# Matmuls of 512 and 256 columns for the mixture of a three-stage kernel, and unbroken runs of its scores and values

## The chip, the cores and the metric

The kernel runs on one core of a Trainium2 chip. TensorE (PE) multiplies, VectorE (DVE), ScalarE (ACT) and GpSimd (POOL) do the work around it, and the queue of SyncE (SP) issues the DMAs. The metric is the device time of one execution in microseconds (us); lower is better. All inputs and outputs are float32 in HBM.

## The reference

Three stages follow one another. Attention with a block mask is computed for 4 batches of 8 heads, 576 tokens and a head size of 64; its 512 values per token go through a layer that takes the largest of three products; and the result goes through four weighted experts, for all 2304 tokens.

```python
scores = scale * np.matmul(q, k.transpose(0, 1, 3, 2))      # 4 x 8 heads, 576 x 576
scores = np.where(block_i >= block_j, scores, -1e9)         # blocks of 64 tokens
attn = np.exp(scores - np.max(scores, axis=-1, keepdims=True))
attn = attn / (np.sum(attn, axis=-1, keepdims=True) + 1e-09)
x = np.matmul(attn, v)                                      # laid out as 2304 x 512
h = np.maximum(np.maximum(x @ w1, x @ w2), x @ w3)          # 2304 x 768, "the mixture"
x = h @ w_out                                               # 2304 x 512
p = domain_probs / (domain_probs.sum(-1, keepdims=True) + 1e-09)
for e in range(4):                                          # 1024 wide each
    out += p[:, e:e + 1] * (np.maximum(x @ e_w1[e], 0.0) @ e_w2[e])
```

## The kernel before, in words

Attention goes by pairs of heads: `NPAIR = 4` pairs for each of the 4 batches, so 16 pairs, numbered from 0. For each pair, `scores` (line 123) multiplies queries by keys in three or four steps; the two heads of a pair lie in the two halves of the partitions (`own = (lo, hi)`), so that a score matmul uses 64 of the array's 128 rows (line 144), and the matmuls of the two heads start nearly together. The last 64 queries of both heads are one matmul of all 128 rows (line 159). DVE finds the smallest score of each row (line 173), ACT takes the exponential with its sum (line 180), POOL divides (line 203, in `normalise`, which is issued one step later). `turn_probs` (line 218) transposes the probabilities on TensorE into PSUM (line 231), DVE and ACT copy them out (line 241). `values` (line 245) multiplies them by the values in 20 matmuls, each of which fills 64 of the 128 output columns of the array (line 263), and ACT copies the two results into `xf` (lines 271 and 272).

PSUM tiles of scores, transposes and values of pairs 4 to 15 share one ring of four banks, `ps_x`.

The mixture of a batch is the generator `moe1(b)` (line 426). Each float32 operand is split into a rounded high and a low part, and a product is three matmuls (`mm3`, line 400): high by high, high by low, low by high. For 18 weight tiles of 128x512 (three matrices by six stretches of 128 columns) and for four of the output matrix it goes over the 576 tokens of the batch in two halves of `CH = 288` columns. A run into one PSUM bank is 12 matmuls for the first kind and 18 for the second. One batch is 18 x 2 x 12 + 4 x 2 x 18 = 576 matmuls. DVE takes the maximum (line 443), POOL splits the hidden values (lines 445, 446). The splits of the inputs, `xh` and `xl`, are made by `moe1_inputs` (lines 423, 424) at the end of the batch's last pair.

The mixture of batch b is laid between the attention of batch b+1: after each step of a pair the main loop calls `filler.upto((at - 1) * UNITS - LAG)`, which issues so many units of `moe1` (a unit is the stretch between two `yield`s). Batch 3 has no attention to lie between; its mixture goes on alone, with the first steps of the experts beside it. The mixture of batch 0 converts its weights on the way (`Convert`, from line 295: ACT, POOL and DVE work on each tile, and a DMA writes the result to `held`); later batches load `held` into five buffers `wt` (512 KB a load) and two buffers `wo` (768 KB).

The order of the instructions on each engine is made by the scheduler of the language, from the program's order and its own view of what is ready; `tc.keep_in_program_order` ties an instruction to the one before that was so marked. The order is fixed before the kernel runs: TensorE takes its instructions one after the other, and one that waits holds up all that stand behind it.

The experts (from line 581 on) follow when the mixture of batch 3 is done: the function `save_tails` (line 648) writes columns 384 to 575 of the mixture's outputs to HBM, and `weights_out` (line 742) loads the experts' second matrices.

Of the kernel before, what the change touches and what calls it, by code (L numbers as in the profile page):

```python
# [15 lines left out]
LAG = 10  # L16
# [11 lines left out]
def program(tc, q, k, v, w123, w_out, probs, e_w1, e_w2, out):  # L28
# [10 lines left out]
    CH = S // 2  # L39
# [38 lines left out]
    for _ in range(4):  # L78
        mp.tile([P, S], F32, name="xf", tag="xf", bufs=4)
# [42 lines left out]

    def scores(n, step):
        pair = pairs[n]
        if step == 0:
# [11 lines left out]
        todo = []  # L137
        for i, at, w, tiles_ in STEPS[step]:
            views = []
            for h in range(2):  # L140
                o = at if isinstance(at, int) else at[h]
                views.append(st[tiles_[h]][:, o:o + w])
            for h in (0, 1) if step == 2 else (1, 0):
                ins = nc.tensor.matmul(  # L144
                    out=views[h], lhsT=qs[own[h], P * i:P * i + P], rhs=ks[own[h], 0:w], start=True, stop=not masked,
                )
                if not masked or len(todo) or h == (step == 2):
                    tc.keep_in_program_order(ins)
            for h in range(2):
                if masked:  # L150
# [4 lines left out]
                todo.append((i, h, views[h]))  # L155
        if step >= 2:
            view = st[-1][:, 192:768]
            for c, n_ in ((0, 320), (320, 256)):
                ins = nc.tensor.matmul(  # L159
                    out=view[:, c:c + n_], lhsT=qs[:, QT:QW], rhs=ks[:, c:c + n_], start=True, stop=True  # L160
                )
                if not masked:
                    tc.keep_in_program_order(ins)
            todo.append((4, 0, view))
        todo.sort(key=lambda x: (step == 0) * x[1])
        done, cols = [], list(range(*COLS[step]))
        for c in range(0, len(cols), 2):
            work = list(zip(cols, todo))[c:c + 2]
            for m, (i, h, x) in work:
                if i < 4 and not masked:  # L170
                    nc.vector.memset(x[lo, x.shape[1] - 64:], 1e30)
            for m, (i, h, x) in work:
                nc.vector.tensor_reduce(mn[:, m:m + 1], x, axis=AX.X, op=ALU.min)  # L173
            for m, (i, h, x) in work:
# [5 lines left out]
                exps.append(nc.scalar.activation(  # L180
                    to, x, ACTF.Exp, bias=mn[:, m:m + 1], scale=-1.0, accum_out=sm[:, m:m + 1],
                ))
                done.append((m, i, to))
# [34 lines left out]
    def turn_probs(g, part):  # L218
# [7 lines left out]
        for n in PARTS[part]:  # L226
# [14 lines left out]
            (nc.scalar.copy if n else nc.vector.tensor_copy)(to, tt[:, 0:c])  # L241
# [3 lines left out]
    def values(n):  # L245
        pair = pairs[n]
        eh, e4, vraw = pair["eh"], pair["e4"], pair["vraw"]
        pool, tag = (ps_v, "v") if n < NPAIR else (ps_x, "x")
        pv = [pool.tile([P, 512], F32, name=f"pv{i}", tag=tag) for i in range(2)]
        ins = None  # L250
        for j in range(5):
            for to, of in ((1, 0), (1, 1), (0, 0)):
                if j and to == 0 or j == 4 and of == 0:
                    continue
                for h in (1, 0):
# [11 lines left out]
                    if old is not None:  # L267
                        tc.keep_in_program_order(ins)
        made["pv"] = ins
        xf = pair["xf"] = mp.tile([P, S], F32, name="xf", tag="xf", bufs=4)  # L270
        nc.scalar.copy(xf[:, 0:P], pv[0][:, 0:P])
        nc.scalar.copy(xf[:, P:S], pv[1][:, 0:S - P])

    def weigh(n, behind):
# [8 lines left out]
        nc.vector.tensor_tensor(pair["xf"][:, 0:512], rt, pair["xf"][:, 0:512], op=ALU.mult)  # L283
# [5 lines left out]
    for n, src in enumerate(tiles):  # L289
        A = src.shape[1]  # L290
        step = A if A <= 4 else A // 2
        pieces += [(n, slice(a, a + step)) for a in range(0, A, step)]

    class Convert:
# [14 lines left out]
        def home(self, n):  # L309
            A = tiles[n].shape[1]  # L310

            tag, bufs = ("wo", 2) if n >= 3 * NF or n in (WT, WT + 1) else ("wt", WT)
            return mp.tile([P, 2, A, P], F32R, name=tag, tag=tag, bufs=bufs)
# [72 lines left out]
    def moe_weight(b, n, tag, bufs):  # L386
# [3 lines left out]
        else:  # L390
            A = tiles[n].shape[1]
            wt = mp.tile([P, 2, A, P], F32R, name=tag, tag=tag, bufs=bufs)
# [21 lines left out]
    def moe1_inputs(b, ds):  # L414
        if b not in xs:
            xs[b] = (
                mp.tile([P, KD, S], F32R, name="xh", tag="xh"),
                mp.tile([P, KD, S], F32R, name="xl", tag="xl"),
            )
        xh, xl = xs[b]  # L420
        for d in ds:
            xf = pairs[b * NPAIR + d]["xf"]
            nc.scalar.copy(xh[:, d], xf)
            nc.vector.tensor_tensor(xl[:, d], xf, f(xh[:, d]), op=ALU.subtract)

    def moe1(b):
        xh, xl = xs[b]
        hh = mp.tile([P, NF, S], F32R, name="hh", tag="hh")
        hl = mp.tile([P, NF, S], F32R, name="hl", tag="hl")
        for ff in range(NF):  # L430
            prev = [None, None]
            for n in range(3):
                wh, wl = moe_weight(b, 3 * ff + n, "wt", WT)
                for c in range(2):
                    cs = slice(c * CH, (c + 1) * CH)
                    m = ps_m.tile([P, 512], F32, name="m", tag="m")
                    yield from mm3(m[:, 0:CH], [(wh[:, d], wl[:, d], xh[:, d, cs], xl[:, d, cs]) for d in range(KD)])
                    t = prev[c]
                    if t is None:
                        t = prev[c] = mp.tile([P, CH], F32, name="mt", tag="mt", bufs=3)  # L440
                        nc.scalar.copy(t, m[:, 0:CH])
                    else:
                        nc.vector.tensor_tensor(t, m[:, 0:CH], t, op=ALU.max)  # L443
                    if n == 2:
                        nc.gpsimd.tensor_scalar(hh[:, ff, cs], t, 1.0, 0.0, op0=ALU.mult, op1=ALU.add)
                        nc.gpsimd.tensor_tensor(hl[:, ff, cs], t, f(hh[:, ff, cs]), op=ALU.subtract)
                    yield
        for d in range(KD):
            wh, wl = moe_weight(b, 3 * NF + d, "wo", 2)
            for c in range(2):  # L450
                cs = slice(c * CH, (c + 1) * CH)
                m = ps_m.tile([P, 512], F32, name="m", tag="m")
                yield from mm3(m[:, 0:CH], [(wh[:, ff], wl[:, ff], hh[:, ff, cs], hl[:, ff, cs]) for ff in range(NF)])
                nc.scalar.copy(x2f[b][:, d, cs], m[:, 0:CH])
                yield
# [794 lines left out]
```

## Time and profile before

| | us |
|---|---|
| median of 3 runs | 1239.15 |
| lowest and highest | 1237.73, 1239.34 |
| the profiled execution | 1239.25 |
| its span, first to last instruction | 1237.1 |
| TensorE busy | 1209.7 (98%) |
| DVE, ACT, POOL busy | 824.2, 455.6, 289.8 |

The profile is one execution. A busy matmul in it is counted until its result has drained, and matmuls overlap, so the busy share says that TensorE hardly stood still, not that each matmul was as short as it can be. How long a matmul holds the array is read from the time between its start and the next one's. The granted clock is a share of 2.4 GHz.

### The profile page before, as it was taken

To read this page: it belongs to the slowest core of one execution; us is meant where nothing else is said; L and a number is where in the kernel's file an instruction comes from. 1 tells how busy PE (TensorE), PEld (TensorE's weight loads), DVE (VectorE), ACT (ScalarE), POOL (GpSimd) and SP (SyncE) were. 2 spreads that over 40 slices of the span, in tenths; PEclk is the share of its full clock that TensorE was granted. 3 is DMA by queue.
4 is the path that set the end of the run, shared out by engine and by line. 5 is a ranking of instruction groups with operands and counts; after the bars stand their busy time and mean duration, and the time that the engine had idled before them with its cause. 6 is when DMAs were issued, how large, how long until landed. Compare 5 with 4: busy or idle time off the path is not lost.

```text
span 1237.1 us, 19744 instructions
## 1 busy us (share of the span) xinstructions
PE 1209.7 (98%) x7681; PEld 1119.4 (90%) x7681; DVE 824.2 (67%) x1453; ACT 455.6 (37%) x964; POOL 289.8 (23%) x360
## 2 busy tenths in 40 slices
PE   7799999999999999999999999999999999999998
PEld 4468888888888999999999998999999999999998
DVE  5756674434333544478888895768787888586896
ACT  6765555334333421333444450233232223222222
POOL 3447663334233022342433440000000000000000
PEclk8899999999999999999999999999999999999999
DMA  7635575443433487679887864867888887676664
GB/s 269 226 113 186 170 249 170 147 138 119 138 116 103 129 299 271 223 289 334 315 311 285 326 239 149 315 252 296 331 301 317 317 312 267 251 267 225 251 214 168
DMA packets 82352, 290.75 MB, mean 235 GB/s; under 512 B 8716, under 2 KB 18004, under 8 KB 69204
## 3 DMA queue, kind: packets, MB, share of 16 engines
q1 hardware_dynamic: 82260, 289.51, 66.1%
q8 instruction: 60, 0.98, 0.3%
q14 instruction: 32, 0.26, 0.1%
HBM read 206.34 MB, written 83.14 MB: 234 GB/s over the span
## 4 chain that ended last, share of the span: by engine, by line
PE 88%; DVE 3%; DMA 3%; ACT 2%; POOL 2%; issue 1%; SPq 0%; DVEq 0%; ACTq 0%; POOLq 0%
PE m L761 26%; PE m L405 24%; PE o L920 17%; PE pv L263 3%; PE o L843 3%; PE o L847 3%; PE o L846 3%; PE st L144 3%; PE tt L231 3%; PE m L920 2%; PE st L159 1%; ACT p L180 1%; DMA w<-kb 1%; DMA arena<-in_w 1%; DVE mn L173 1%
## 5 line engine op out<-in xcount | busy, mean ns | idle before, releaser
L405 PE MATMUL m<-xh,wt 128*128 128x288 f32 x1120 | 246.1, 303 | 0.0
L761 PE MATMUL m<-t,w 128*128 128x384 f32 x1152 | 227.8, 336 | 0.0
L920 PE MATMUL o<-hx,w 128*128 128x384 f32 x1176 | 226.1, 337 | 0.5 <-DMA w<-kb 0.5
L920 PEld LDWEIGHTS o<-hx,w 128*128 128x128 f32 x1176 | 207.9, 188 | 0.8 <-PE m L761 0.8
L761 PEld LDWEIGHTS m<-t,w 128*128 128x128 f32 x1152 | 203.4, 188 | 2.4
L405 PEld LDWEIGHTS m<-xh,wt 128*128 128x128 f32 x1120 | 184.2, 188 | 10.8 <-issue 6.3
L761 PE MATMUL m<-b,w 128*128 128x384 f32 x864 | 175.2, 336 | 2.2 <-ACT tmp L786 1.6
L405 PE MATMUL m<-xl,wt 128*128 128x288 f32 x560 | 164.9, 294 | 0.0
L761 PEld LDWEIGHTS m<-b,w 128*128 128x128 f32 x864 | 153.0, 188 | 5.9 <-ACT tmp L786 1.9
L405 PEld LDWEIGHTS m<-xl,wt 128*128 128x128 f32 x560 | 105.3, 188 | 0.3
L180 ACT ACTIVATE p<-st,mn 128x128 f32<-128x128 f32 (+2 forms) x144 | 78.3, 554 | 63.1 <-DVE mn L173 62.9
L443 DVE TENSOR_TENSOR mt<-m,mt 128x288 f32<-128x288 f32 x96 | 42.8, 452 | 88.0 <-PE m L405 87.7
L781 DVE TENSOR_TENSOR tmp<-m,tmp 128x384 f32<-128x384 f32 x144 | 77.9, 549 | 19.5 <-PE m L761 19.1
L173 DVE TENSOR_REDUCE mn<-st 128x1 f32<-128x128 f32 (+2 forms) x144 | 70.0, 515 | 30.5 <-PE st L151 15.5
L203 POOL TENSOR_SCALAR p<-p,sm 128x128 f32<-128x128 f32 (+4 forms) x112 | 65.1, 600 | 101.0 <-ACT e L241 45.2
L405 PE MATMUL m<-hh,wo 128*128 128x288 f32 x384 | 81.2, 299 | 0.3 <-DMA wo<-held 0.2
L891 ACT CAST hx<-hq 128x768 fp32r<-128x768 f32 x49 | 40.6, 836 | 99.0 <-PE o L920 74.4
L843 PE MATMUL o<-w,hh 128*128 128x512 f32 x192 | 74.7, 391 | 0.2 <-ACT hh L821 0.2
L846 PE MATMUL o<-w,hh 128*128 128x512 f32 x192 | 74.6, 390 | 0.0
L847 PE MATMUL o<-w,hl 128*128 128x512 f32 x192 | 74.4, 391 | 0.0
L231 PE MATMUL tt<-ident,p 128*128 128x128 f32 x400 | 60.7, 282 | 11.0 <-ACT p L180 6.1
L716 POOL TENSOR_TENSOR w<-part,w 128x512 fp32r<-128x512 f32 x32 | 49.5, 1568 | 88.1 <-ACT w L714 68.3
(143 smaller groups left out, 1886.9 us busy)
## 6 DMA issues: line engine op xcount, KB each, us to landing
w<-kb SPq DMA_DIRECT2D x55, 1024.0 KB, 6.0
w<-ka SPq DMA_DIRECT2D x30, 1792.0 KB, 8.3
ka<-w SPq DMA_DIRECT2D x16, 1792.0 KB, 6.7
wt<-held SPq DMA_DIRECT2D x54, 512.0 KB, 4.0
kb<-part SPq DMA_DIRECT2D x16, 1024.0 KB, 6.9
kb<-w SPq DMA_DIRECT2D x16, 768.0 KB, 4.8
arena<-in_w SPq DMA_DIRECT2D x18, 512.0 KB, 3.8
wo<-held SPq DMA_DIRECT2D x12, 768.0 KB, 4.4
```

Source lines behind the costliest of these rows:

```text
L173: nc.vector.tensor_reduce(mn[:, m:m + 1], x, axis=AX.X, op=ALU.min)
L180: exps.append(nc.scalar.activation(to, x, ACTF.Exp, bias=mn[:, m:m + 1], scale=-1.0, accum_out=sm[:, m:m + 1],))
L203: normal.append(nc.gpsimd.tensor_scalar(x, x, sm[:, c:c + 1], 1.0, op0=ALU.mult, op1=ALU.mult))
L231: nc.tensor.transpose(tt[:, c:c + P], pt[i][:, k0:k0 + P], ident)
L405: nc.tensor.matmul(out=out_, lhsT=w, rhs=x, start=m == 0, stop=m == n - 1)
L716: eng.tensor_tensor(w[:, a:b, 1], raw[:, a:b], f(w[:, a:b, 0]), op=ALU.subtract)
L761: ins = nc.tensor.matmul(out=m, lhsT=a, rhs=b, start=start and n == 0, stop=stop and n == 3 * KH - 1, skip_group_check=True,)
L781: nc.vector.tensor_tensor(t, x, y, op=ALU.add)
L843: ins = nc.tensor.matmul(out=o, lhsT=hh[:, ts], rhs=wh, start=i == 0, stop=False)
L846: nc.tensor.matmul(out=o, lhsT=hh[:, ts], rhs=wl, start=False, stop=False)
L847: nc.tensor.matmul(out=o, lhsT=hl[:, ts], rhs=wh, start=False, stop=i == G - 1)
L920: nc.tensor.matmul(out=o, lhsT=a, rhs=b, start=start and m == 0, stop=stop and m == 2, skip_group_check=True,)
```

## The change

The mixture no longer halves the 576 tokens of a batch. It goes over the first `MAIN = 512` in one run; the last `REST = 64` tokens of each batch are split by `moe1_inputs` into tiles `rest_x` that hold all four batches (256 columns), and `moe1(3)` multiplies them beside batch 3's own 512: each weight tile of batch 3 is used for a run of 512 and then a run of 256. Their hidden values lie in `rest_h` and in two buffers that were weight buffers (`wu`), so batch 3 takes weights into `wt` (three) and `wo` (two). `xf` has no tile of its own any more: it lies in the part of `arena` that will hold batch 3's outputs. `mm3` yields after 4 matmuls and not after 6, and `UNITS` and `LAG` follow.

For pairs 4 to 15, the first matmul of a step of scores and of a pair's values gets added dependencies (`whole`): on the instructions that empty the PSUM banks which all of the run will need (`busy`, and `c_ends` for the wide score tile), and for the values on all copies of the transposed probabilities (`turned`). The rest of the run is issued under `tc.high_priority()`.

```diff
-LAG = 10
+LAG = 9
...
+    MAIN = 512
+    REST = S - MAIN
     for x in ("xh", "xl"):
-        mp.tile([P, KD, S], F32R, name=x, tag=x)
-    hidden = [mp.tile([P, NF, S], F32R, name=x, tag=x) for x in ("hh", "hl")]
+        mp.tile([P, KD, MAIN], F32R, name=x, tag=x)
...
+    rest_x = [mp.tile([P, KD, B * REST], F32R, name=f"rx{i}", tag=f"rx{i}") for i in range(2)]
+    rest_h = mp.tile([P, 2, 2, B * REST], F32R, name="rh", tag="rh")
...
+    XB = 4
+    x_ends, c_ends = [], []
+
+    def whole(ins, ends):
+        for x in ends:
+            tc.add_manual_dep(
+                ins.ins, x.ins.name, mybir.DependencyInfo(mybir.DependencyClass.Sync, mybir.DependencyReason.DATA),
+                reason="a run begins when all of it can",
+            )
+
+    def busy(count):
+        at = len(x_ends)
+        return [x for n in range(max(0, at - XB), at + count - XB) for x in x_ends[n]]
+
     def scores(n, step):
         pair = pairs[n]
+        before = busy(KINDS[step].count("x")) + (c_ends[-1] if c_ends and "c" in KINDS[step] else [])
...
+                if n >= NPAIR and not todo and h == (step != 2):
+                    whole(ins, before)
+                    rest.enter_context(tc.high_priority())
...
+        before = busy(2) + pair["turned"]
         pv = [pool.tile([P, 512], F32, name=f"pv{i}", tag=tag) for i in range(2)]
...
+                    elif n >= NPAIR:
+                        whole(ins, before)
+                        rest.enter_context(tc.high_priority())
+        rest.close()
         made["pv"] = ins
-        xf = pair["xf"] = mp.tile([P, S], F32, name="xf", tag="xf", bufs=4)
...
+        xf = pair["xf"] = x2f[B - 1][:, n % NPAIR]
...
+            if b == B - 1 and not wide and n % WT >= 3:
+                wide = True
+                taken[0] += 1
+            wt = weight_tile(n, wide)
             nc.sync.dma_start(out=f(wt[:].rearrange("p k a f -> p k (a f)")), in_=held[n][:, :, 0:A * P])
...
-                if m % 6 == 0 and m < n:
+                if m % 4 == 0 and m < n:
                     yield
 
-    UNITS = 3 * NF * 2 * 2 + KD * 2 * 3
+    UNITS = 3 * NF * 3 + KD * 5
...
         for d in ds:
             xf = pairs[b * NPAIR + d]["xf"]
-            nc.scalar.copy(xh[:, d], xf)
-            nc.vector.tensor_tensor(xl[:, d], xf, f(xh[:, d]), op=ALU.subtract)
+            rs = slice(b * REST, (b + 1) * REST)
+            for cs, h, l in (
+                (slice(0, MAIN), xh[:, d], xl[:, d]), (slice(MAIN, S), rest_x[0][:, d, rs], rest_x[1][:, d, rs]),
+            ):
+                nc.scalar.copy(h, xf[:, cs])
+                nc.vector.tensor_tensor(l, xf[:, cs], f(h), op=ALU.subtract)
...
+        runs = [(MAIN, "mt", *xs[b], *hs, lambda d: x2f[b][:, d, 0:MAIN])]
+        if b == B - 1:
+            room = [rest_h] + [mp.tile([P, 2, 2, B * REST], F32R, name="wu", tag="wu", bufs=2) for _ in range(2)]
+            hs = [[x[:, i, j] for x in room for j in range(2)] for i in range(2)]
+            runs.append((B * REST, "mr", *rest_x, *hs, lambda d: whole[:, d, :, MAIN:S]))
         for ff in range(NF):
-            prev = [None, None]
+            prev = [None] * len(runs)
             for n in range(3):
-                wh, wl = moe_weight(b, 3 * ff + n, "wt", WT)
-                for c in range(2):
-                    cs = slice(c * CH, (c + 1) * CH)
-                    m = ps_m.tile([P, 512], F32, name="m", tag="m")
-                    yield from mm3(m[:, 0:CH], [(wh[:, d], wl[:, d], xh[:, d, cs], xl[:, d, cs]) for d in range(KD)])
+                wh, wl = moe_weight(b, 3 * ff + n)
+                for c, (w, tag, xh, xl, hh, hl, _) in enumerate(runs):
+                    m = ps_m.tile([P, 512], F32, name="m", tag="m")[:, 0:w]
+                    yield from mm3(m, [(wh[:, d], wl[:, d], xh[:, d], xl[:, d]) for d in range(KD)])
```

How the instructions stand on TensorE around the values of pair 9, in the attention of batch 2: `pv` is the values' result, `m` a run of the mixture, `tt` a tile of transposes, `st` scores. Before:

```order
L263 MATMUL pv_2909<-e_2623,vraw 64x64 x2
L263 MATMUL pv_2909<-eh,vraw 64x256 x2
L405 MATMUL m<-xh,wt 128x288
...
L405 MATMUL m<-xh,wt 128x288
L263 MATMUL pv_2909<-e_2623,vraw 64x64 x2
L263 MATMUL pv_2909<-eh,vraw 64x128 x2
L263 MATMUL pv_2909<-e_2623,vraw 64x64 x4
L405 MATMUL m<-xh,wt 128x288
```

And now (line 292 is what line 263 was, 452 is 405, 257 is 231, 165 is 144):

```order
L452 MATMUL m<-xh,wu 128x512
L292 MATMUL pv_2423<-eh,vraw 64x384 x2
L292 MATMUL pv_2423<-e_2224,vraw 64x64 x2
L292 MATMUL pv_2422<-eh,vraw 64x128 x2
L292 MATMUL pv_2423<-eh,vraw 64x384 x2
L292 MATMUL pv_2423<-e_2224,vraw 64x64 x2
L292 MATMUL pv_2423<-eh,vraw 64x256 x2
L292 MATMUL pv_2423<-e_2224,vraw 64x64 x2
L292 MATMUL pv_2423<-eh,vraw 64x128 x2
L292 MATMUL pv_2423<-e_2224,vraw 64x64 x4
L257 MATMUL tt<-ident,p_2380 128x128 x4
```

The 12 matmuls of the mixture that stood inside the values are gone from there, and the transposes of the next pair follow the values at once.

TensorE where batch 1's attention ends and the mixture of batch 1 begins. Before:

```order
L263 MATMUL pv_2218<-e_1880,vraw 64x64 x4
L405 MATMUL m<-hl,wo 128x288
...
L231 MATMUL tt<-ident,p_2134 128x128 x4
...
L405 MATMUL m<-hl,wo 128x288
...
L144 MATMUL st<-raw 128x128 x2
```

And now:

```order
L292 MATMUL pv_1911<-e_1649,vraw 64x64 x4
L257 MATMUL tt<-ident,p_1850 128x128 x4
L257 MATMUL tt<-ident,p_1698 128x128
L257 MATMUL tt<-ident,p_1696 128x128
L257 MATMUL tt<-ident,p_1698 128x128 x2
L165 MATMUL st<-raw 128x128 x2
L165 MATMUL st<-raw 128x384 x2
L257 MATMUL tt<-ident,p_1858 128x128 x2
L452 MATMUL m<-xh,wt 128x512 x2
L257 MATMUL tt<-ident,p_1863 128x128 x4
L452 MATMUL m<-xl,wt 128x512
```

Before, the output products of batch 0 (`hl,wo`) stood between these; now none is left, and the first matmuls after the values are two of batch 1's mixture that need the high part of its last pair.

The queue of SP at the end of the mixture of batch 3: `wo<-held` loads an output weight tile, `xt` is what `save_tails` writes, `part` is the first load of an expert's second matrix. Before:

```order
L393 DMA wo<-held_97 128x1536
L653 DMA xt_4897<-arena 128x2x192
L393 DMA wo<-held_98 128x1536
L653 DMA xt_4897<-arena 128x2x192
L653 DMA xt_4899<-arena 128x2x192
L745 DMA part<-in_e_w 128x1024
```

And now:

```order
L440 DMA wo<-held_97 128x1536
L708 DMA xt_3893<-arena 128x2x192
L708 DMA xt_3894<-arena 128x2x192
L440 DMA wo<-held_98 128x1536
L708 DMA xt_3893<-arena 128x2x192
L708 DMA xt_3894<-arena 128x2x192
L708 DMA xt_3895<-arena 128x2x192
L708 DMA xt_3896<-arena 128x2x192
L800 DMA part<-in_e_w 128x1024
```

Four of the eight writes stood in the attention of batch 2 before; now all eight stand here, six of them ahead of the load of `part`.

## Rows read from the trace of the kernel before

**Rows 1.** Busy time by stage: us, PE DVE ACT POOL, clock, DMA share, GB/s

```profile
77.00:419.00 342.00, 341.82 (x2662) 299.14 (x2659) 162.48 (x380) 151.38 (x414) 145.00 (x218) 1.00 0.47 149
...
107.00:137.00 30.00, 29.91 (x232) 25.57 (x231) 18.96 (x38) 16.09 (x42) 21.07 (x27) 1.00 0.52 174
```

**Rows 2.** Timeline of TensorE in batch 3's output products: start, us, instruction

```profile
424.01 0.29 PE L405 MATMUL m<-hl,wo 128*128 128x288 f32 x1
...
426.79 0.30 PE L405 MATMUL m<-hl,wo 128*128 128x288 f32 x1
```

**Rows 3.** Timeline of TensorE in the experts, 512 columns

```profile
559.16 0.39 PE L843 MATMUL o<-w,hh 128*128 128x512 f32 x1
...
562.56 0.39 PE L843 MATMUL o<-w,hh 128*128 128x512 f32 x1
```

**Rows 4.** Timeline of TensorE around broken values, pair 13

```profile
362.75 0.29 PE L405 MATMUL m<-xh,wt 128*128 128x288 f32 x1
362.96 0.87 PE L263 MATMUL pv<-eh,vraw 128*64 128x384 f32 x4
...
364.75 0.60 PE L263 MATMUL pv<-eh,vraw 128*64 128x256 f32 x4
365.29 0.41 PE L405 MATMUL m<-xh,wt 128*128 128x288 f32 x1
365.53 0.30 PE L405 MATMUL m<-xl,wt 128*128 128x288 f32 x1
```

**Rows 5.** Timeline of TensorE, values of pairs 1 and 3, no mixture beside

```profile
47.56 0.87 PE L263 MATMUL pv<-eh,vraw 128*64 128x384 f32 x4
...
74.81 0.87 PE L263 MATMUL pv<-eh,vraw 128*64 128x384 f32 x4
...
76.60 0.60 PE L263 MATMUL pv<-eh,vraw 128*64 128x256 f32 x4
77.04 0.28 PE L263 MATMUL pv<-e,vraw 128*64 128x64 f32 x4
...
77.37 0.40 PE L263 MATMUL pv<-e,vraw 128*64 128x64 f32 x8
77.70 0.66 PE L280 MATMUL rt<-ident,arena 128*128 128x128 f32 x4
78.20 1.04 PE L231 MATMUL tt<-ident,p 128*128 128x128 f32 x8
```

**Rows 6.** Timeline of TensorE, scores of pair 14 and the next mixture run

```profile
357.13 1.56 PE L144 MATMUL st<-raw 64*128 64x512 f32 x8
...
359.51 0.48 PE L405 MATMUL m<-xh,wt 128*128 128x288 f32 x1
```

**Rows 7.** Timeline of POOL after these scores

```profile
364.87 3.01 POOL L203 TENSOR_SCALAR p<-p,sm 128x512 f32<-128x512 f32 x5 [0.42 <-DVE sm L188]
```

**Rows 8.** Groups by shape: busy us, mean ns, idle before

```profile
L203 POOL TENSOR_SCALAR p<-p,sm 128x512 f32<-128x512 f32 x24 | 17.1, 723 | 15.2 <-DVE sm L188 12.7 <-ACT arena L331 1.8 <-ACT eh L241 0.6
...
L241 ACT COPY eh<-tt 128x512 f32<-128x512 f32 x32 | 18.8, 587 | 21.1 <-PE tt L231 21.1
...
L272 ACT COPY xf<-pv 128x448 f32<-128x448 f32 x16 | 8.6, 536 | 24.6 <-PE pv L263 24.6
```

**Rows 9.** Chain of waits while batch 0's weights are converted: start, us, what

```profile
100.01 2.10 POOL p L203 x3
...
109.25 0.33 PE tt L231
```

**Rows 10.** Chain of waits at the end of batch 3's mixture

```profile
494.55 4.65 DMA wo<-held
499.34 9.79 PE m L405 x72
509.13 3.14 PE m L761 x18
```

**Rows 11.** Timeline of SP's queue there

```profile
505.24 0.46 SPq L745 DMA_DIRECT2D part<-in_e_w  x1
```

More of the change, by code (lines that the diff above doesn't have):

```diff
@@ L121, in program @@
     COLS = ((0, 4), (4, 6), (6, 9), (4, 9))
+    XB = 4
[9 more added lines that the diff above has]
+        return [x for n in range(max(0, at - XB), at + count - XB) for x in x_ends[n]]
     def scores(n, step):
         pair = pairs[n]
+        before = busy(KINDS[step].count("x")) + (c_ends[-1] if c_ends and "c" in KINDS[step] else [])
+        ends = [[] for _ in KINDS[step]]
+        for x, end in zip(KINDS[step], ends):
+            (x_ends if x == "x" else c_ends).append(end)
         if step == 0:
@@ L154, in scores @@
                     ))
-                todo.append((i, h, views[h]))
+                todo.append((i, h, views[h], ends[tiles_[h]]))
         if step >= 2:
@@ L182, in scores @@
                 ))
+                end.append(exps[-1])
                 done.append((m, i, to))
@@ L240, in turn_probs @@
                 to = pair["eh"][h][:, o:o + w].rearrange("x s c -> x (s c)")
-            (nc.scalar.copy if n else nc.vector.tensor_copy)(to, tt[:, 0:c])
+            x_ends.append([(nc.scalar.copy if n else nc.vector.tensor_copy)(to, tt[:, 0:c])])
+            pair.setdefault("turned", []).append(x_ends[-1][0])
         if part == 1 and h == 0:
@@ L268, in values @@
                         tc.keep_in_program_order(ins)
+                    elif n >= NPAIR:
+                        whole(ins, before)
+                        rest.enter_context(tc.high_priority())
+        rest.close()
         made["pv"] = ins
-        xf = pair["xf"] = mp.tile([P, S], F32, name="xf", tag="xf", bufs=4)
-        nc.scalar.copy(xf[:, 0:P], pv[0][:, 0:P])
-        nc.scalar.copy(xf[:, P:S], pv[1][:, 0:S - P])
+        xf = pair["xf"] = x2f[B - 1][:, n % NPAIR]
+        ends = [nc.scalar.copy(xf[:, 0:P], pv[0][:, 0:P]), nc.scalar.copy(xf[:, P:S], pv[1][:, 0:S - P])]
+        if n >= NPAIR:
+            x_ends.extend([x] for x in ends)
     def weigh(n, behind):
@@ L292, in program, with weight_tile @@
         pieces += [(n, slice(a, a + step)) for a in range(0, A, step)]
+    taken = [0]
+    def weight_tile(n, wide):
+        if wide:
+            tag, bufs = "wo", 2
+        else:
+            tag, bufs = (("wt", 3), ("wu", WT - 3))[taken[0] % WT >= 3]
+            taken[0] += 1
+        return mp.tile([P, 2, tiles[n].shape[1], P], F32R, name=tag, tag=tag, bufs=bufs)
     class Convert:
@@ L391, in moe_weight @@
             A = tiles[n].shape[1]
-            wt = mp.tile([P, 2, A, P], F32R, name=tag, tag=tag, bufs=bufs)
+            if b == B - 1 and n == 0:
+                taken[0] = 0
+            wide = n >= 3 * NF
+            if b == B - 1 and not wide and n % WT >= 3:
+                wide = True
+                taken[0] += 1
+            wt = weight_tile(n, wide)
             nc.sync.dma_start(out=f(wt[:].rearrange("p k a f -> p k (a f)")), in_=held[n][:, :, 0:A * P])
@@ new lines, in moe1 @@
+    def moe1(b):
+        hidden = [mp.tile([P, NF, MAIN], F32R, name=x, tag=x) for x in ("hh", "hl")]
+        whole = arena.rearrange("p (b d s) -> p d b s", b=B, d=KD)
+        hs = [[x[:, ff] for ff in range(NF)] for x in hidden]
+        runs = [(MAIN, "mt", *xs[b], *hs, lambda d: x2f[b][:, d, 0:MAIN])]
[3 more added lines that the diff above has]
+            runs.append((B * REST, "mr", *rest_x, *hs, lambda d: whole[:, d, :, MAIN:S]))
@@ L450, in moe1 @@
[L450 to L454, printed above, removed]
+            wh, wl = moe_weight(b, 3 * NF + d)
+            for w, _, _, _, hh, hl, to in runs:
+                m = ps_m.tile([P, 512], F32, name="m", tag="m")[:, 0:w]
+                yield from mm3(m, [(wh[:, ff], wl[:, ff], hh[ff], hl[ff]) for ff in range(NF)])
+                x = to(d)
+                nc.scalar.copy(x, m if len(x.shape) == 2 else m.rearrange("p (b s) -> p b s", b=B))
```

41 lines of the change are left out of this document (18 added, 23 removed).

## Prediction

> **What bounds the kernel now.** I read the page first, then the stages by window, then TensorE's timeline, start against start. TensorE bounds nearly all of it. From 77 to 419 us, where the attention of batches 1 to 3 lies between the mixture of batches 0 to 2, it is busy for 341.82 of 342 us at the full granted clock, while DVE, ACT and POOL are busy for less than half [rows 1]. That alone doesn't say that matmuls are dense, so I took the time from one start to a later one. In a run of the mixture 21 matmuls of 288 columns take 426.79 - 424.01 = 2.78 us, 132.4 ns each [rows 2]; 288 columns at 2.4 GHz are 120 ns, so 12.4 ns come on top of each. With 512 columns, in the experts, 15 take 562.56 - 559.16 = 3.40 us, 226.7 ns each, 13.4 ns over the 213.3 of their columns [rows 3]. The excess hardly grows with the width, so it belongs to the instruction. Fewer, wider matmuls on the same columns are worth it.
>
> **The change part by part.** *The mixture's matmuls.* Before: 4 x 576 = 2304 of 288 columns, 2304 x 132.4 ns = 305.0 us. Now: 4 x (18 x 12 + 4 x 18) = 1152 of 512 columns, 1152 x 226.7 = 261.2 us, and 288 of 256 columns, which no row of mine shows. Bounds for those: 106.7 ns, the columns alone, and 132.4, the row of 288. On the line through 288 and 512 (0.421 ns a column) they take 119 ns, which I use: 34.3 us (30.7 to 38.1). The sum falls by 9.5 us (5.7 to 13.1).
>
> TensorE: Matmul & The Clock Gate, a page of the Trainium skill, speaks against this in its section on the back-to-back issue gap: warm, it gives N/2.4 + 2.5 ns from start to start, and 864 matmuls fewer would then give 2.2 us. The trace doesn't agree: its gaps are 12 to 13 ns over N/2.4.
>
> Where this falls matters. In the attention stretch stood 1656 matmuls of 288 before the last values, now 846 of 512: 219.3 against 191.8 us, 27.5 less. Behind the last values stood 648, 85.8 us; now 306 of 512 and 288 of 256, 103.7 us, 17.9 more. The gain exists only if the stretch really shrinks.
>
> *The breaks.* Scores with 64 rows and values with 64 columns use part of the array, and passing between them and the mixture costs time. Entering: 362.96 - 362.75 = 0.21 us where a mixture matmul takes 0.13, so 0.08 or 0.09. Leaving: 365.29 - 364.75 = 0.54 us for the four matmuls that take 0.44 (77.04 - 76.60) inside an unbroken run, 0.10 more; and the first matmul behind takes 0.24 and not 0.13, 0.11 more [rows 4, 5]. Leaving to transposes also costs some 0.10 in front (0.33 us from the last eight to the next, the same as to the mixture), and the four behind take 0.50 us where the rate of the eight after them, (1.04 - 0.28)/7 = 0.109, makes 0.44: 0.16 in all [rows 5]. In the order of the instructions I counted, between the first mixture matmul and the last values: entries 54 before and 37 now; exits to the mixture 42 and 1; exits to transposes 2 and 25. So 17 x 0.09 + 41 x 0.21 - 23 x 0.16 = 1.5 + 8.6 - 3.7 = 6.4 us less. If leaving to transposes cost as much as to the mixture, 5.3; if nothing, 10.
>
> *The added waits.* The first matmul of a run now waits for every bank and copy that the run needs. Behind it on TensorE stand the run, the transposes after it and all of the mixture, and ACT, DVE and POOL in turn wait for these. Three places decide.
> First, the transposes straight behind the values: they need the first probabilities that POOL divides. From the start of the scores to that: 364.87 - 357.13 + 0.72 = 8.5 us [rows 6 to 8]. TensorE now comes there after 2.4 us of scores (359.51 - 357.13), 15 or 19 mixture matmuls (3.4 or 4.3 us) and unbroken values, 77.70 - 74.81 = 2.9 us [rows 5]: 8.7 to 9.6 us. It just fits; nothing.
> Second, the two batch ends without mixture left (after pairs 7 and 11). The next mixture matmul needs the values copied by ACT (0.54 us, with a smaller copy ahead) and rounded (about 0.6, as ACT's 512-wide copy of 587 ns) [rows 8]: some 1.7 us after the values. TensorE has 8 transposes, scores and 2 more transposes to do meanwhile, 0.9 + 1.1 + 0.2 us. The scores wait for the same copies, 0.2 to 0.5 us: 1 us for both ends.
> Third, batch 0, where the conversion shares POOL: 21.07 of 30 us busy [rows 1], and the chain passes from POOL to a transpose there [rows 9]. With a period shorter by a tenth POOL is at 77%. I take 1.5 us for the four pairs; the bounds are 0 and one such POOL piece of 2.1 us a pair, 8.4.
> Waits together: 2.5 us, from 0 to about 9.5.
>
> *Batch 3 and the hand-over.* Each weight tile now serves 12 x (0.227 + 0.119) = 4.2 us and not 3.2, and an output tile 6.2 us and not 4.8. The wait of 4.65 us for such a tile, which the chain shows and which held TensorE for some 0.3 us (72 matmuls took 9.79 us and not 9.53) [rows 10], is covered. On SP six writes now stand ahead of the load of `part`; the last of the six waits for the copies of the third output tile. The load went out at 505.24, 3.9 us before the experts' first matmul [rows 10, 11]; now one output tile of 6.2 us still follows, so it goes out earlier, some 5 us before. Nothing on either side. Splitting inputs in two pieces, wider copies and POOL's 512-wide splits lie on engines under half busy: nothing, or part of the waits above.
>
> **Sum.** The profiled execution took 1239.25 us, 2.15 more than its span and 0.1 from the median of 1239.15. 1239.25 - 9.5 - 6.4 + 2.5 = 1225.85: I predict 1226 us. The stretch of 342 us should end near 311, at 26 us a pair.
>
> **Rivals.** *The stretch doesn't shrink (slower).* With 27.5 us less mixture to cover it, attention could be held by its own chain of scores, smallest, exponential, division, transposes, values, since TensorE stands still at every wait. If the stretch kept its 342 us, the tail's 17.9 us would make 1257. It decides from waits of 15.9 us on, 1.3 us a pair, when nothing is left of 9.5 + 6.4. For it: the fit of 8.5 us in 8.7, and POOL in batch 0. Against: pairs 2 and 3, with conversion but no mixture beside, took (74.81 - 47.56)/2 = 13.6 us each [rows 5], half of the 26.
> *Half of the gain is waited away (no change).* Waits of 13 to 18 us, at some of these places in most pairs: 1237 to 1241.
> *256 columns cost as much as 288.* If the weights set the pace of a short matmul, 288 x 13.4 ns = 3.9 us are lost: 1230. Nothing narrower than 288 stands in rows of the split operands to refute it; the excess, still 12.4 at 288, speaks against a floor near there.
> *The excess is not the instruction's.* If the excess of 12.4 ns follows the columns or the reading of both operands, the mixture gains only about 2 us and 1239.25 - 2.2 - 6.4 + 2.5 gives 1233. This is what the page of the Trainium skill cited above amounts to. Both widths in the rows speak against it.
>
> **How the numbers follow.** The forecast, with its waits of 0 to 6 us, gets 0.70 and alone spans 1222 to 1230. The dear 256 columns get 0.08, the excess by columns 0.04, waits of 6 to 13 us 0.05: all still faster. No change, 0.05. The stretch that doesn't shrink, 0.08. The measurement of this kernel tells 0.2%, 2.5 us, from no change. So faster 0.87, same 0.05, slower 0.08. The range of 8 in 10: below, all the gain without waits and with 256 columns at their cheapest, 1239.25 - 13.1 - 6.4 = 1220; I set 1221. Above, 1236: it takes in the dear 256 columns, the excess by columns and waits up to 13 us, and leaves out no change and slower.
>
> **What would show it.** In the profile after: mixture matmuls 227 ns from start to start at 512 columns and about 119 at 256; the last values some 31 us earlier than before and the experts' first matmul some 13; entries into runs 37; no gap over 0.5 us on TensorE in batches 2 and 3 but at the batch ends. The experts should last as long as before. It is wrong if TensorE shows idle time with ACT or POOL as the releaser in each pair, if the last values come less than 18 us earlier, or if 256 columns take 130 ns.

## The result and the profile after

| | before | after |
|---|---|---|
| median, us | 1239.15 | 1226.04 |
| lowest and highest | 1237.73, 1241.8 | 1222.77, 1227.66 |
| the profiled execution, us | 1239.25 | 1226.04 |
| its span, us | 1237.1 | 1224.1 |

Five runs of each; after stands to before as 0.9885, with an interval of 0.9871 to 0.9898. Forecast: 1226 us, 1221 to 1236.

The page of after has this line (busy time, share, instructions):

```profile
PE 1193.8 (98%) x6817; PEld 1057.8 (86%) x6817; DVE 822.8 (67%) x1433; ACT 451.9 (37%) x950; POOL 282.3 (23%) x324
```

TensorE is busy for the same 98%: its work has become shorter, not its pauses fewer. For the stretch in which attention and mixture interleave, with the columns of [rows 1]:

```profile
81.00:387.35 306.35, 304.79 (x1826) 229.68 (x1826) 160.81 (x354) 145.25 (x395) 133.58 (x180) 1.00 0.50 162
```

For the size of the stretch I take its ends from TensorE's timeline. Before, the first matmul of the mixture and the last eight of the last values:

```profile
79.58 0.40 PE L405 MATMUL m<-xh,wt 128*128 128x288 f32 x1
...
422.24 0.40 PE L263 MATMUL pv<-e,vraw 128*64 128x64 f32 x8
```

After, the same two and the matmul behind:

```profile
80.95 0.48 PE L452 MATMUL m<-xh,wt 128*128 128x512 f32 x1
...
389.84 0.40 PE L292 MATMUL pv<-e,vraw 128*64 128x64 f32 x8
390.17 0.50 PE L452 MATMUL m<-hh,wo 128*128 128x512 f32 x1
```

The eight take 0.33 us to the next start, so the stretch ended at 422.57 and ends at 390.17: 343.0 us before, 309.2 now, 33.8 less, and 25.8 us a pair. The end of the mixture is in the chain of waits of after (start, us, what), which answers to [rows 10]:

```profile
387.35 2.89 PE pv L292 x40
390.24 104.59 PE m L452 x594
494.83 3.13 PE m L816 x18
```

The 594 matmuls behind the last values are the 306 and 288 of the forecast. From 390.17 to the experts' 494.83 are 104.7 us; before, from 422.57 to 509.13 [rows 10], 86.6. The stretch gives 33.8, the tail takes 18.1, and 15.7 remain. In the first stage 1.4 us are lost (80.95 for 79.58), and in the experts 1.3 (1224.1 - 494.83 = 729.3 for 1237.1 - 509.13 = 728.0). Together 13.0, the difference of the spans. These are two executions, one of each kernel; the five of after lie between 1222.77 and 1227.66 us, so a difference of 1 us in one stage may be chance.

The price of a matmul, TensorE's timeline of after with 512 columns, which answers to [rows 2] and [rows 3]:

```profile
391.20 0.39 PE L452 MATMUL m<-hl,wo 128*128 128x512 f32 x1
...
393.93 0.39 PE L452 MATMUL m<-hl,wo 128*128 128x512 f32 x1
```

Twelve matmuls in 2.73 us, 227 ns each. With 256 columns:

```profile
443.12 1.60 PE L452 MATMUL m<-rx,wt 128*128 128x256 f32 x12
444.55 0.40 PE L452 MATMUL m<-xh,wt 128*128 128x512 f32 x1
```

1.43 us for twelve, 119 ns each, the value taken from the line through 288 and 512.

The values of pair 9, one of the runs that had been broken as in [rows 4]:

```profile
240.82 0.39 PE L452 MATMUL m<-xh,wu 128*128 128x512 f32 x1
241.14 0.87 PE L292 MATMUL pv<-eh,vraw 128*64 128x384 f32 x4
...
244.03 1.10 PE L257 MATMUL tt<-ident,p 128*128 128x128 f32 x8
244.88 0.48 PE L452 MATMUL m<-xh,wu 128*128 128x512 f32 x1
```

They take 2.89 us in one piece, as pair 3 did without a mixture beside it [rows 5], and the transposes follow without a pause. Entering costs 241.14 - 240.82 - 0.227 = 0.09 us, as before. The eight transposes take 0.85 us. Four that stand inside the mixture take 0.35 (176.07 to 176.42, below), and four more at 0.109 would make it 0.79: behind the values 0.06 us falls on the transposes, as in [rows 5], besides the 0.10 in front.

The waits that I found on TensorE from the first to the last matmul of the mixture are in batch 0:

```profile
88.56 0.27 PE L257 MATMUL tt<-ident,p 128*128 128x128 f32 x1
89.40 0.50 PE L452 MATMUL m<-xh,wt 128*128 128x512 f32 x1 [0.57 <-ACT mt L496]
...
176.07 0.60 PE L257 MATMUL tt<-ident,p 128*128 128x128 f32 x4
176.42 0.48 PE L452 MATMUL m<-hh,wo 128*128 128x512 f32 x1
177.65 0.66 PE L257 MATMUL tt<-ident,p 128*128 128x128 f32 x4 [0.74 <-ACT p L205]
178.55 0.44 PE L257 MATMUL tt<-ident,p 128*128 128x128 f32 x2 [0.25 <-ACT p L205]
178.95 0.50 PE L452 MATMUL m<-hh,wo 128*128 128x512 f32 x1
```

Start against start, less what the instructions themselves take, that is 0.8 us at 89.40 and 1.5 us from 176.42 to 178.95. The second lies at the end of the conversion. In the timeline of ACT there:

```profile
176.12 0.57 ACT L372 ACTIVATE arena<-arena 128x384 int32<-128x384 uint32 x1 [1.24 <-POOL arena L384]
...
177.41 0.19 ACT L205 ACTIVATION_READ_ACCUMULATOR p<-st,mn 128x1 f32 x1
```

The transposes at 177.65 start when ACT has taken an exponential (177.41 + 0.19). It reads scores from a bank of the ring that the transposes share, and POOL divides its result only from 179.12 on, so the wait is for the bank. ACT came to its exponentials late, since a step of the conversion stood ahead of them and waited 1.24 us for POOL. At the end of batch 1, where the order of the instructions leaves no mixture over, nothing waits:

```profile
193.12 1.09 PE L257 MATMUL tt<-ident,p 128*128 128x128 f32 x8
194.15 1.14 PE L165 MATMUL st<-raw 64*128 64x128 f32 x8
195.22 0.44 PE L257 MATMUL tt<-ident,p 128*128 128x128 f32 x2
195.41 0.71 PE L452 MATMUL m<-xh,wt 128*128 128x512 f32 x2
```

From the values' end to the first matmul that needs them are 193.12 to 195.41, 2.29 us, and the work between fills them. The end of batch 2 reads the same.

SP's queue, the load named in [rows 11]:

```profile
490.44 0.47 SPq L800 DMA_DIRECT2D part<-in_e_w  x1
```

It goes out 4.4 us before the experts' first matmul; before, 3.9.

### The profile page after: what moved, and what is told of

Read it like the earlier page. It is cut to its first block, busy times and chain, and to the rows that moved or that the text cites. A ratio compares the mean times of both kernels' runs of the same rounds, so it can differ in the third digit from the quotient of the medians.

```text
span 1224.1 us, 17918 instructions
## 1 busy us (share of the span) xinstructions
PE 1193.8 (98%) x6817; PEld 1057.8 (86%) x6817; DVE 822.8 (67%) x1433; ACT 451.9 (37%) x950; POOL 282.3 (23%) x324
## 4 chain that ended last, share of the span: by engine, by line
PE 72%; DVE 9%; DMA 8%; ACT 5%; POOL 4%; issue 3%; SPq 0%; POOLq 0%; DVEq 0%; ACTq 0%
PE m L816 22%; PE m L452 20%; PE o L975 17%; DMA t<-in_e_w 4%; PE pv L292 2%; PE tt L257 2%; PE st L165 2%; DMA part<-in_e_w 2%; PE m L975 2%; ACT p L205 2%; POOL arena L384 1%; PE o L898 1%; POOL p L229 1%; PE o L902 1%; PE o L901 1%
## 5 line engine op out<-in xcount | busy, mean ns | idle before, releaser
L452 PE MATMUL m<-xh,wt 128*128 128x512 f32 x352 | 118.5, 398 | 0.6 <-ACT mt L496 0.6
L229 POOL TENSOR_SCALAR p<-p,sm 128x128 f32<-128x128 f32 (+4 forms) x112 | 67.8, 622 | 72.7 <-DVE sm L214 38.3
L452 PEld LDWEIGHTS m<-xh,wt 128*128 128x128 f32 x352 | 65.7, 188 | 13.8 <-ACT mt L496 0.9
L257 PEld LDWEIGHTS tt<-ident,p 128*128 128x128 f32 x400 | 47.2, 146 | 30.9 <-POOL p L229 8.9
L498 DVE TENSOR_TENSOR mt<-m,mt 128x512 f32<-128x512 f32 x48 | 33.0, 687 | 58.5 <-PE m L452 56.9
L771 POOL TENSOR_TENSOR w<-part,w 128x512 fp32r<-128x512 f32 x32 | 50.1, 1590 | 91.5 <-ACT w L769 91.5
L452 PE MATMUL m<-xl,wt 128*128 128x512 f32 x176 | 69.2, 393 | 0.0
L452 PE MATMUL m<-hh,wo 128*128 128x512 f32 x192 | 63.6, 399 | 0.0
```

Of the source, the lines that this page charges most:

```text
L229: normal.append(nc.gpsimd.tensor_scalar(x, x, sm[:, c:c + 1], 1.0, op0=ALU.mult, op1=ALU.mult))
L257: nc.tensor.transpose(tt[:, c:c + P], pt[i][:, k0:k0 + P], ident)
L771: eng.tensor_tensor(w[:, a:b, 1], raw[:, a:b], f(w[:, a:b, 0]), op=ALU.subtract)
```

## The experiments

First the prices. *Narrower matmuls of the mixture in the kernel before*, thirds of 192 columns, 3456 matmuls where there were 2304 (`UNITS`, `LAG` and the buffers of `mt` follow, here and, as far as they have to, in the next two):

```diff
-    CH = S // 2
+    CH = S // 3
...
-                for c in range(2):
+                for c in range(3):
```

> The kernel before with the mixture in thirds of 192 columns: 3456 matmuls in place of 2304 on the same columns. My theory, some 12 ns to each matmul: the line through 288 and 512 gives 92 ns at 192, 318 us in place of 305, 13 us more; breaks (entries 64, exits 46 and 7) 2.5 us more: 1254 to 1255 us. Rival, the excess follows the columns: 1241 to 1242. Rival, below some width the loading of weights sets the pace, at the 109 ns between two transposes: 3456 x 0.109 = 377 us, 1313.

Measured: 1319.33 us, 1.0644 [1.0631, 1.0658]. A miss for the straight line; the rival with the floor, 1313, came near. TensorE's timeline in batch 3:

```profile
499.89 0.27 PE L405 MATMUL m<-xl,wt 128*128 128x192 f32 x1
...
502.90 0.27 PE L405 MATMUL m<-xl,wt 128*128 128x192 f32 x1
```

27 matmuls in 3.01 us, 111.5 ns each, where the line says 92. And 3456 x 111.5 ns = 385.3 us are 80.3 more than the 305.0 of before: 1319.5. Below 256 columns another thing than the columns sets the pace.

*The rest of each batch by itself*, 64 columns beside the batch's own 512, and not 256 in batch 3, which now takes its weights as the other batches do:

```diff
-        if b == B - 1:
...
+        rs = slice(b * REST, (b + 1) * REST)
+        runs.append((REST, "mr", rest_x[0][:, :, rs], rest_x[1][:, :, rs], *hs, lambda d: x2f[b][:, d, MAIN:S]))
```

> The changed kernel with the last 64 tokens of a batch multiplied in that batch, as a run of 64 columns behind each run of 512, and not all four batches' together as 256 columns beside batch 3: 1152 matmuls of 64 columns in place of 288 of 256. My theory of a price for each matmul: the line gives 38 ns at 64 columns, 44 us in place of 34.5, and breaks 21 exits to the mixture and 5 to transposes in place of 1 and 25, 1 us more: 1236 us. Rival, a short matmul is paced by its weights: at the 109 ns between transposes 126 us, so 1318.

Measured: 1317.57 us, 1.0634 [1.0619, 1.0648]; a miss again, and the rival with the floor right. From TensorE's timeline:

```profile
500.43 1.42 PE L447 MATMUL m<-rx,wu 128*128 128x64 f32 x12
501.69 0.48 PE L447 MATMUL m<-xh,wt 128*128 128x512 f32 x1
```

Twelve take 1.26 us here, the middle value over all of them is 112 ns. So 64 columns cost what 192 cost. Gathering the rests of four batches, 1152 matmuls of 64 into 288 of 256, is worth about 1152 x 112 - 288 x 119 ns = 95 us by these prices, and 1317.57 - 1226.04 = 91.5 us by the runs; without it the whole change would be a loss.

*The 512 as two runs of 256*, else as in after:

```diff
+        HALF = MAIN // 2
...
+        for c in range(2):
+            cs = slice(c * HALF, (c + 1) * HALF)
```

> The changed kernel with each run of 512 columns as two runs of 256 on the same columns (LAG 18, with units half as wide): 2304 matmuls of 256 in place of 1152 of 512, and the same 288 of 256. Breaks: 37 entries as in the changed kernel, 19 exits to the mixture (1) and 7 to transposes (25), 18 x 0.21 - 18 x 0.16 = 0.9 us more. Theory, a price of some 12 to 13 ns for each matmul on top of its columns, seen as 120 ns at 256 and 227 at 512: 2304 x 0.120 - 1152 x 0.2267 = 15.3 us more, so 1242. Rival, the excess over the columns goes with the columns: 1227. Rival, runs of 256 columns are slower beside each other than beside 512, near the 111 ns and 12 to 13 on top: 1250 or more.

Measured: 1241.25 us, 1.0019 [1.0006, 1.0032], as expected: slower than before. From TensorE's timeline:

```profile
445.20 0.28 PE L452 MATMUL m<-xh,wo 128*128 128x256 f32 x1
...
448.08 1.60 PE L452 MATMUL m<-rx,wo 128*128 128x256 f32 x12
449.52 0.28 PE L452 MATMUL m<-xh,wt 128*128 128x256 f32 x1
```

24 matmuls in 2.88 us and 12 in 1.44: 120 ns. So two of them take 2 x 120 - 227 = 13 ns more than one of 512, which is the excess of [rows 2] and [rows 3], taken by an edit and not from a slope; 1152 times that are 15.0 us. The whole kernel lost 1241.25 - 1226.04 = 15.2 us (16.6 by the ratios), with a schedule that also differs at the breaks (19 exits to the mixture, where after has 1) and that waits longer (TensorE's waits over the mixture sum to 3.4 us in the profile's account of them, in after to 1.6). The total thus bears out the size, and the 13 ns rest on the starts. The Trainium skill, TensorE: Matmul & The Clock Gate, gives 2.5 ns over N/2.4 in its section on the back-to-back issue gap, with which these matmuls would have cost 2.9 us more. The section calls this the gap of a single matmul and says that in a stream of weight loads and matmuls, as here, both set the spacing; the measurement decides against 2.5 ns for these matmuls.

Then the two halves of the change apart. *The unbroken runs alone*, in the kernel before with its two times 288:

```diff
+                if n >= NPAIR and not todo and h == (step != 2):
+                    whole(ins, before)
...
+        before = busy(2) + pair["turned"]
...
+                    elif n >= NPAIR:
+                        whole(ins, before)
```

> The kernel before with the added dependencies of scores and values alone; the mixture keeps its halves of 288 columns, its LAG of 10 and its tile xf. In the order of TensorE's instructions between the first mixture matmul and the last values, runs are entered 37 times (before 54, after 37) and left to the mixture 22 times (42; 1), to transposes 4 times (2; 25). My theory, a price for each break: 17 x 0.09 + 20 x 0.21 - 2 x 0.16 = 5.4 us less, less some 0.5 of waits: 1234 us. Rival, the added waits eat what the breaks gave: 1239. Rival, the breaks are nearly all of the change's 13 us: 1228.

Measured: 1236.21 us, 0.9977 [0.9968, 0.9986]: faster, by 3 us, less than expected. The scores and values became shorter by 5.9 us (table below). The 22 exits to the mixture that stayed were part of the expectation; what it lacked were waits like this one, in TensorE's timeline of this kernel:

```profile
424.73 0.37 PE L437 MATMUL m<-hh,wo 128*128 128x288 f32 x1 [1.61 <-DMA wo<-held]
```

At 87.77 the mixture waits another 0.98 us for ACT, and it begins at 81.25 us where before has 79.58 (the last section says why).

*The wide matmuls alone*, after without the dependencies:

```diff
-                    whole(ins, before)
-                    rest.enter_context(tc.high_priority())
+                    pass
```

> The changed kernel without its added dependencies: runs of 512 and 256 columns, scores and values broken up by the scheduler as before. Entries 63 (before 54), exits to the mixture 41 (42), to transposes 11 (2). My theory, 12 to 13 ns for each matmul left out: 9.4 us less for the matmuls, 9 x 0.09 + 9 x 0.16 = 2.2 us more for breaks, so 1232 us. Rival, the excess over the columns follows the columns: 2.2 less and 2.2 more, 1239. Rival, the stretch needs the runs to shrink at all: not below 1239.

Measured: 1243.36 us, 1.0033 [1.002, 1.0047]. The clearest miss: all of the wide matmuls are in this kernel, and it is slower than before. The two parts bring -3 and +4 us alone and -13 together. TensorE's timeline of this kernel shows it at the scores of a pair:

```profile
340.93 1.12 PE L165 MATMUL st<-raw 64*128 64x512 f32 x2
341.99 0.50 PE L450 MATMUL m<-xl,wt 128*128 128x512 f32 x1
...
345.37 1.55 PE L165 MATMUL st<-raw 64*128 64x512 f32 x6
346.85 1.24 PE L182 MATMUL st<-raw 128*128 128x320 f32 x4
347.74 0.58 PE L450 MATMUL m<-xh,wt 128*128 128x512 f32 x1
```

Two score matmuls of one head go out at 340.93, and mixture follows until 345.37, when the other head's come with the rest of the step. The first piece holds TensorE for 1.06 us. What is left takes 347.74 - 345.37 = 2.37 us, and the whole step with both heads took 2.38 [rows 6]. The two that went ahead are thus paid in full on top: each head uses 64 rows, and together they had run side by side. I counted 18 such separated steps in the order of the instructions, 8 of them with 512 columns; the other ten have 128, and such a piece takes 0.41 us (357.31 to 357.73 in this timeline). 8 x 1.06 + 10 x 0.41 = 12.6 us, most of the 13.8 by which the scores and values of this kernel exceed those of after (table below).

*The dependencies on the scores alone*, and *on the values alone*; each is after with the lines of the other left out as above:

> The changed kernel with the added dependencies on the scores alone; the values have none. No matmul of one head's scores stands apart from the other head's in the order (in the kernel with 512 columns and no dependencies, which took 1243, 18 pairs of heads are separated by mixture). Entries 45 (changed kernel 37), exits to the mixture 9 (1), to transposes 25 (25). Theory, the separated heads were what made that kernel slow: 8 x 0.09 + 8 x 0.21 = 2.4 us over the changed kernel's 1226: 1228. Rival, only the number of breaks counts: 1243 less 18 x 0.09 + 32 x 0.21 - 14 x 0.16 = 6.1: 1237.

Measured: 1229.1 us, 0.9916 [0.9903, 0.9929], as expected.

> The changed kernel with the added dependencies on the values alone; the scores have none. 21 pairs of heads are separated again, 9 of them of 512 columns. Entries 58, exits to the mixture 34, to transposes 13. Theory of the separated heads: 1226 and 21 x 0.09 + 33 x 0.21 - 12 x 0.16 = 6.9 us for breaks and some 7 us for matmuls that no longer run beside the other head's (9 x 0.52, 10 x 0.2): 1240. Rival, breaks alone: 1233.

Measured: 1241.88 us, 1.0016 [1.0006, 1.0026], as expected, though the 0.52 us that the expectation took for a separated head of 512 columns is half of what the step at 340.93 shows. Against the wide matmuls alone, the dependencies on the scores bring 14.3 us and those on the values 1.5, which is not clear of the noise (the intervals overlap); behind the scores the values bring another 3.1. Before had its own median beside each series, 1238.95 to 1240.21 us; by the ratios these are 14.5, 2.1 and 3.8.

*The two heads kept together and nothing else*: the first score matmul waits for the banks of its own two heads, not for those of the whole step, and the values wait as before.

```diff
-        before = busy(KINDS[step].count("x")) + (c_ends[-1] if c_ends and "c" in KINDS[step] else [])
+        before = busy(2 if step != 2 else 1) + (c_ends[-1] if c_ends and step == 2 else [])
```

> The kernel with 512 columns in which the first score matmul of a step waits for the banks of its two heads and for nothing more, and the values have no added dependency. Two pairs of heads (256 columns) are still separated. Entries 46, exits to the mixture 15, to transposes 20. Theory of the separated heads: 1226 and 9 x 0.09 + 14 x 0.21 - 5 x 0.16 = 2.9, and 0.4 for the two: 1229. Rival, breaks alone: 1243 less 17 x 0.09 + 26 x 0.21 - 9 x 0.16 = 5.6: 1238.

Measured: 1230.11 us, 0.9927 [0.991, 0.9944], as expected. That is 13.3 of the 14.3 us: it is enough that two heads start together, and the 1.0 us that waiting for the whole step adds is within the noise. In the profiles the stretch of the table is shorter by 13.3 us too. The scores and values give 9.6 of it and the mixture 5.8, since every head that stands alone also makes an entry and an exit of its own (17 entries and 26 exits to the mixture fewer); the transposes take 1.9 back. (The profiled execution of this kernel, 1235.74 us, was the longest of its six: its mixture begins at 83.70 us, and its experts take longer too.)

*More of the mixture kept back* for the places where transposes or a batch's end might wait:

```diff
-LAG = 9
+LAG = 14
```

> The changed kernel with LAG 14 in place of 9: the mixture is issued five units (20 matmuls, 4.5 us) later beside attention, so that more of it is left at the ends of the batches. The breaks are the same (37, 1, 25). Theory, the trace of the changed kernel shows no wait at the batch ends, so nothing is gained: 1225 to 1227. Rival, the mixture that has run out there costs 1 us at each of two ends: 1224.

Measured: 1226.2 us, 0.9891 [0.9875, 0.9908], the time of after: the waits in batch 0 are there as in after, and there was none at the ends of the batches that more mixture would have covered.

The stretch from the first to the last matmul of the mixture, with TensorE's time divided by what started at each start (worked out from the timelines, in us), and the breaks as counted in the order of the instructions:

| kernel | stretch | scores, values | transposes | mixture | entries / exits to mixture / to transposes |
|---|---|---|---|---|---|
| before | 429.4 | 79.7 | 27.7 | 321.9 | 54 / 42 / 2 |
| unbroken runs alone | 425.0 | 73.8 | 29.7 | 321.5 | 37 / 22 / 4 |
| wide matmuls alone | 432.1 | 87.9 | 28.3 | 316.0 | 63 / 41 / 11 |
| values alone | 430.8 | 87.8 | 29.5 | 313.5 | 58 / 34 / 13 |
| scores alone | 416.3 | 77.5 | 30.3 | 308.6 | 45 / 9 / 25 |
| heads together | 418.8 | 78.3 | 30.2 | 310.2 | 46 / 15 / 20 |
| after | 413.7 | 74.1 | 30.4 | 309.2 | 37 / 1 / 25 |

The separated heads stand in the second column: 88 us where 18 and 21 steps are separated, 74 to 80 elsewhere (before has one such step, the heads together two).

## Why the prediction was right, step by step

The total came out within 0.1 us of the forecast. So close it is by luck: the five runs spread over 5 us, and misses of opposite sign cancel. The range and the mechanism are not luck; the steps came out as follows.

*The mixture's matmuls, forecast -9.5.* Right. 1152 x 227 + 288 x 119 ns = 295.8 us, for 305.0: -9.2. (By the mean of all matmuls between two others of the mixture, 229 ns at 512 columns and 133 at 288, it is -8.2, and the remainder below would be 1 us larger.) The excess is the instruction's: 13 ns from two of 256 against one of 512. The dear 256 columns are refuted, but narrowly. The line that priced them ends right below: 192 and 64 columns take 111.5 and 112 ns, so 256, at 119, stand just above a floor that the forecast held for unlikely because the excess was still 12.4 at 288. That reason proved nothing on the floor.

*The breaks, forecast -6.4.* The counts came out as read from the order, with one exit to the mixture. The stretch lost 15.7 us, 9.2 of them by the matmuls; 6.5 remain for breaks and waits together. With 0.9 us more of waits (next step) the breaks are worth -7.4, a remainder and not a measurement. The prices themselves came out as in the rows: 0.09 for entering, 0.06 on the transposes behind the values. What the counts leave out is that before has a step with its heads apart, too. TensorE's timeline of before:

```profile
140.15 1.12 PE L144 MATMUL st<-raw 64*128 64x512 f32 x2
141.21 0.40 PE L405 MATMUL m<-xh,wt 128*128 128x288 f32 x1
```

This piece holds TensorE for 1.06 us, and after has none like it. That would account for the 1.0 us between forecast and remainder, but it was not tried by itself.

*The waits, forecast +2.5.* Mis-sized, within its bounds. In batch 0, forecast 1.5, there are 2.3 us; the conversion on POOL is behind the larger of the two, but by way of ACT, whose exponentials it held up, and not of POOL's division. At the two batch ends, forecast 1.0, there is nothing: I had put 1.7 us beside 2.2 of work and still charged for the scores. Before had some 1.4 us of its own, at the transpose of [rows 9], near 181 us and at the load of [rows 10], which the sum had not set against it: net +0.9.

*The hand-over, forecast 0.* The load of `part` goes out 4.4 us ahead and the wait for `wo` is gone. But the first stage lasts 1.4 us longer and the experts 1.3. Neither was foreseen. The first comes from a fourth place where an added wait acts, which the forecast put at nothing (last section). Of the second I don't know the cause, and it may be none: over the eleven profiled kernels the experts last from 726.7 to 731.3 us. They and the smaller waits cancel: -9.2 - 7.4 + 0.9 + 1.4 + 1.3 = -13.0.

*What was tacitly wrong: that the parts add.* The forecast took the gain of the mixture and the gain of the unbroken runs for two terms, each against the kernel before. From that came my expectation of 1232 us for the wide matmuls alone; they took 1243.36. With them and without the dependencies the schedule separates the two heads in 18 steps, and the scores and values rise from 79.7 to 87.9 us. So the dependencies are worth 3 us in the kernel before and 17.3 in this one. The forecast's total did not suffer, since it counted breaks in the order of the changed kernel itself, where no head stands alone. Why the schedule separates so many heads there, and with 288 columns only one step, was not tried. The added priority has no share: without it, every engine gets the same instructions with the same waits in the same order.

*The rivals.* The stretch that keeps its 342 us: refuted, 309. The gain waited away: 2.3 us of waits, and more mixture in reserve changes nothing. (13 us of waits would have made 1236.4 and not 1237.) The excess by columns, to whose 2.2 us the rule of the Trainium skill cited above also comes: refuted by the 13 ns for each matmul of the 256-column halves.

## What to carry to other kernels

Price a matmul at two widths from one start to the next, and measure the narrow one before planning on it: the line broke right below the width that this change uses. Price the parts of a change in the order of the changed kernel, not each against the old one; here the widened matmuls are a loss until the two heads' matmuls are tied together. A matmul on half of the rows is cheap only beside its partner, so look in the order for any that stands alone. An added wait acts wherever its instruction stands, also in the stage ahead of the one it is meant for.

## What the hardware showed that was not expected

Mixture matmuls of 64 and of 192 columns both start every 112 ns, of 256 every 119 to 120, of 288 every 132, of 512 every 227.

The change also acts in the first stage. Pair 4 is the first whose scores have added dependencies, and these scores are issued beside pair 3, ahead of the mixture. TensorE's timeline of after:

```profile
73.32 0.70 PE L165 MATMUL st<-raw 64*128 64x256 f32 x4 [0.95 <-ACT p L205]
...
73.98 1.72 PE L183 MATMUL st<-raw 128*128 128x320 f32 x4
75.63 1.55 PE L292 MATMUL pv<-eh,vraw 128*64 128x384 f32 x4
```

And of before:

```profile
72.98 0.70 PE L144 MATMUL st<-raw 64*128 64x256 f32 x4 [0.40 <-ACT p L180]
73.65 1.24 PE L159 MATMUL st<-raw 128*128 128x320 f32 x4
```

What they wait for are two exponentials of the step ahead, which end with these instructions on ACT. After:

```profile
72.41 0.19 ACT L205 ACTIVATION_READ_ACCUMULATOR p<-st,mn 128x1 f32 x1
...
73.07 0.20 ACT L205 ACTIVATION_READ_ACCUMULATOR p<-st,mn 128x1 f32 x1
```

And before the first of the two:

```profile
72.74 0.19 ACT L180 ACTIVATION_READ_ACCUMULATOR p<-st,mn 128x1 f32 x1
```

ACT is earlier in after, by 0.33 us. But the scores start behind the second exponential (73.07 + 0.20), where before they started behind the first (72.74 + 0.19). In the seven kernels with dependencies on the scores this wait is 0.91 to 1.07 us, in the four without 0.28 to 0.40: it is the dependency's.

Behind it the granted clock is lower. Windows of after and of before, with the columns of [rows 1]:

```profile
72.00:80.00 8.00, 7.05 (x55) 4.23 (x56) 3.27 (x9) 3.87 (x13) 2.81 (x6) 0.79 0.25 78
```

```profile
72.00:80.00 8.00, 7.45 (x69) 5.25 (x70) 4.79 (x12) 5.30 (x16) 4.42 (x9) 1.00 0.37 112
```

A mean of 0.79 means that TensorE ran in part at 1.2 GHz. The wide scores then take 1.65 us for 1.16 from start to start, and the values 4.04 (75.63 to 79.67) for 2.89. That makes 1.6 us for the lower clock and 0.55 for the longer wait. Some 0.8 of it come back, since after is 0.2 us ahead at the step before and begins the mixture ahead of the next scores; 1.4 stay.

The pause by itself does not make the clock fall. With the dependencies on the scores alone there is the same pause, and the clock over 72 to 80 us is 0.99. TensorE's timeline of that kernel:

```profile
75.01 0.70 PE L165 MATMUL st<-raw 64*128 64x256 f32 x4 [0.91 <-ACT p L205]
```

There the clock was low ahead of the pause, by its windows:

```profile
68.00:72.00 4.00, 3.45 (x12) 1.79 (x13) 1.99 (x5) 2.95 (x11) 0.93 (x2) 0.60 0.07 26
```

What decides where it falls, no run settles.
